# Second phase of a three-stage network in pairs of blocks, with one planned list of operations for both late phases

## The chip, the cores and the metric

The kernel runs on one core of a Trainium2 chip. The metric is the device time of one execution in microseconds (us). Below, PE is TensorE (the matmuls), DVE is VectorE, ACT is ScalarE, POOL is GpSimd, and SP is the engine that issues the transfers.

## The reference

Three stages follow each other. The first is a recurrent attention over 4 batches, 8 heads, 768 positions and 48 channels. Its output, as 3072 tokens of 384 numbers, goes through four experts, each weighted by a probability of the token; the result goes through one more two-layer network with a gate.

```python
p = domain_probs / (domain_probs.sum(-1, keepdims=True) + 1e-09)
for e in range(4):                       # w1: 4 x 384 x 1024, w2: 4 x 1024 x 384
    h = np.maximum(x @ w1[e], 0.0)
    out += p[:, e:e + 1] * (h @ w2[e])
h = out @ w_in                           # 384 x 2048
g = h * np.clip(h + 3.0, 0.0, 6.0) / 6.0
return g @ w_out                         # 2048 x 384
```

w_in and w_out arrive as 64-bit floats.

## The kernel before, in words

**Products.** Every factor is split into a high part and a low part, and a product is three matmuls: high times high, high times low, low times high. A matmul takes 128 rows and 512 tokens.

**Blocks and slices.** The tokens lie in 6 blocks of 512 (NB), the hidden columns in slices of 256 (SL), 16 for the experts and 8 for the last network. The **first phase** does the attention and, in an order written out by hand, the first 7 slices (S0) of the experts for every block, and puts the sums of each expert into DRAM (acc_d). Its last steps, those of block 5, are the tail. The **second phase** does the other 9 slices of the experts (1 of expert 1, 4 each of experts 2 and 3). The **third phase** does the 8 slices of the last network.

**Second phase, block by block.** The loop over steps_ takes one block, one slice and one half of 128 hidden columns at a time, 108 steps. mm1 issues 9 matmuls into ph (line 987), ACT makes the high part of the relu (line 997), DVE the low part (line 1004), and mm2 issues the 9 matmuls of the step before into three sums po (line 1038). After the last step of an expert, finish multiplies each sum by the probability (line 1077) and adds it to the block's accumulator acc (line 1082), both on DVE; add_acc1 (line 1065, DVE) adds what the first phase left. The finished block is stored as x2_d (line 1084).

**The decode.** decode (from line 813) turns w_in and w_out into 32-bit floats in 48 jobs of 256 columns, a job in two steps of the second phase: six DVE instructions (lines 847, 849, 853, 860, 861, 862), and on GpSimd a square (line 848) and an add (line 863).

**Third phase, pairs of blocks.** It takes two blocks at once with a scheme that forms a 2x3 by 3x2 product of tiles with 11 products in place of 12. group is one slice of one pair: 11 products into two PSUM banks, chain_a and chain_b (line 1388), which hold running sums, and 36 second-layer matmuls into six sums pq (line 1432), 69 in all. A chain is copied out on ACT (copied, line 1392) or added to the copy on DVE (summed, line 1396); the gate is four instructions, ACT, DVE, ACT, DVE (lines 1403, 1407, 1416, 1419). The inputs have to be prepared. Sums and differences of the two blocks' tiles (prepare_x, lines 1331 to 1336) and of the weight quarters (prepare_w, lines 1271 to 1274) are made on GpSimd. High parts are made on ACT (lines 1281, 1290, 1350), low parts on DVE (lines 1283, 1292, 1352). Prepared weights are stored in DRAM (ws_d) for the first pair and fetched for the others. The place of each of these in the order is a time written out by hand (at_u), in units of three matmuls, 23 to a group.

**Order.** Each engine works its instructions in the order in which they are issued, and waits in that order. SP issues the loads and stores, GpSimd stands in the same order of issue.

Of the kernel before, what the change touches and what calls it, by code (L numbers as in the profile page):

```python
# [720 lines left out]
def tile_gla__then__moe__then__moe2(  # L721
# [41 lines left out]
    SB = 4  # L763
# [4 lines left out]
    xp = ctx.enter_context(tc.tile_pool(name="xp", bufs=2))  # L768
    rawp = ctx.enter_context(tc.tile_pool(name="rawp", bufs=2))
    wpa = ctx.enter_context(tc.tile_pool(name="wpa", bufs=S0))  # L770
    hp = ctx.enter_context(tc.tile_pool(name="hp", bufs=2))
    gp = ctx.enter_context(tc.tile_pool(name="gp", bufs=2))
    dram = ctx.enter_context(tc.tile_pool(name="dram", bufs=1, space=bass.MemoryType.DRAM))
# [39 lines left out]
    def decode():  # L813

        CW = 256
        big = f32_of((1151 << 20) - 1)
        tiny = f32_of(897 << 20)
        ve = nc.vector  # L820
        jobs = []
        for src, dst in ((w_in, w_in32), (w_out, w_out32)):
            s_ = src.bitcast(I32).rearrange("(p r) c -> p (r c)", p=P)
            d_ = dst.rearrange("(p r) c -> p (r c)", p=P)
            jobs += [(s_, d_, c) for c in range(d_.shape[1] // CW)]
        raws_ = {}

        def load(x):
            if x < len(jobs):
                s_, _, c = jobs[x]  # L830
                raws_[x] = dp.tile([P, CW, 2], I32, tag="raw", bufs=2, name=f"raw_{x}")
                nc.sync.dma_start(raws_[x].rearrange("p n w -> p (n w)"), s_[:, 2 * CW * c : 2 * CW * (c + 1)])

        load(0)
        load(1)
        for _ in range(3):
            yield
        last = None
        for x, (_, d_, c) in enumerate(jobs):
            if x:  # L840
                load(x + 1)
            raw = raws_.pop(x)
            hi, lo = raw.bitcast(F32)[:, :, 1], raw.bitcast(U32)[:, :, 0]
            hc = dp.tile([P, CW], F32, tag="hc", name=f"hc_{x}")
            sq = dp.tile([P, CW], F32, tag="sq", name=f"sq_{x}")
            a = dp.tile([P, CW], F32, tag="a", bufs=2, name=f"a_{x}")
            ve.tensor_scalar(hc, hi, big, -big, op0=ALU.min, op1=ALU.max)  # L847
            nc.gpsimd.tensor_tensor(sq, hc, hc, op=mul)  # L848
            ve.tensor_scalar(
                a.bitcast(I32), hc.bitcast(I32), 3, 0x3FFFFFF8,  # L850
                op0=ALU.logical_shift_left, op1=ALU.bitwise_and,
            )
            ve.scalar_tensor_tensor(
                a.bitcast(I32), hc.bitcast(I32), -0x40000000, a.bitcast(I32),
                op0=ALU.bitwise_and, op1=ALU.bitwise_or,
            )
            if last:
                nc.sync.dma_start(*last)
            yield
            ve.scalar_tensor_tensor(a, sq, tiny * tiny, a, op0=ALU.is_ge, op1=mul)  # L860
            ve.tensor_scalar(hc.bitcast(I32), a.bitcast(I32), -0x800000, None, op0=ALU.bitwise_and)
            ve.scalar_tensor_tensor(hc, lo, 2.0**-52, hc, op0=mul, op1=mul)
            nc.gpsimd.tensor_tensor(a, a, hc, op=add)
            last = (d_[:, CW * c : CW * (c + 1)], a)
            yield
        nc.sync.dma_start(*last)


# [23 lines left out]
    for b in range(NBLK):  # L892
        phase_visits(1, b, S0, S1)
# [8 lines left out]
    def rw(nm):  # L902
        nonlocal nraw
        if early:
            return early.pop(0)
        nraw += 1
        pool = rawq if late and nraw % 3 == 0 else rawp
        return pool.tile([P, 3 * SL], F32, tag="rw", name=nm)
# [21 lines left out]
    def round_w(y, i):  # L930
        raw = raws.pop((y, i))
        pool = wpb if S0 <= i < S0 + SB else wpa
        hi, lo = (pool.tile([P, 3 * SL], F32R, tag=f"w{y}{z}", name=f"w{y}{z}_{i}") for z in "hl")
# [6 lines left out]

    def load_x(phase, n):
        raw = rw(f"rx_{phase}_{n}").rearrange("p (k t) -> p k t", k=KT)
        nc.sync.dma_start(raw, x_d[:, :, n * U : n * U + U])
        raws[(phase, n, "x")] = raw
# [19 lines left out]
    hts, accs, pbs, acc = {}, {}, {}, {}  # L964
    late, rawq = False, None
    halfs, pair, plan = 0, None, {}

    def mm1(vi, f):
# [29 lines left out]
        if plan is not None:  # L998
            plan[(vi, f)] = high
        else:  # L1000
            high()
# [8 lines left out]
    def mm2(vi, f, held=False):  # L1010
# [10 lines left out]
        elif first:  # L1021
            nonlocal ps2
            if ps2 is None:
                ps_ctx.close()
                ps2 = ctx.enter_context(tc.tile_pool(name="ps2", bufs=3, space=PSUM, reuse_waits="tile"))
            second = vv["phase"] == 1 and vi % 2
            pools = [(psa, "psa") if second else (ps2, "ps2") for m in range(KT)]
            accs[vi] = [pool.tile([P, 512], F32, tag=tag, name=f"po_{vi}_{m}") for m, (pool, tag) in enumerate(pools)]
        terms = ((wh, hh), (wl, hh), (wh, hl))
        spans = ((0, 1), (2,)) if half and not last else ((0, 1, 2),)  # L1030
        for m, os in [(m, os) for os in spans for m in range(KT)]:
# [7 lines left out]
            if last and plan is None and not held and (m > 0 or not half):  # L1039
                for x in (0, 1) if half and m == 1 else (m,):  # L1040
                    finish(vi, x)
# [11 lines left out]
    def load_acc(b):  # L1053
        acc[b] = sp.tile([P, KT, NB], F32, tag="acc", name=f"acc_{b}")
        nc.sync.dma_start(acc[b], acc_d[0][:, :, b * NB : (b + 1) * NB])

    def load_acc1(e, n):
        raw = rw(f"ra{e}_{n}").rearrange("p (k t) -> p k t", k=KT)
        nc.sync.dma_start(raw, acc_d[e][:, :, n * U : n * U + U])
        raws[(e, n, "a")] = raw  # L1060

    def add_acc1(e, n):
        b, c = n * U // NB, n * U % NB
        a = acc[b][:, :, c : c + U]
        nc.vector.tensor_tensor(a, a, raws.pop((e, n, "a")), op=add)

    def finish(vi, m):
# [3 lines left out]
        b, t0 = vv["b"], vv["b"] * NB + vv["lo"]  # L1071
        pb = pbs[vi][:, 0:n]
        if vv["phase"] == 0 and m == KT - 1:
            t = pbs[vi]
        else:
            t = gp.tile([P, 512], F32, tag="t", name=f"t_{vi}_{m}")
        nc.vector.tensor_tensor(t[:, 0:n], po[:, 0:n], pb, op=mul)
        if vv["phase"] == 0:
            after(2, lambda: nc.sync.dma_start(acc_d[vv["e"]][:, m, t0 : t0 + n], t[:, 0:n]))
            return  # L1080
        a = acc[b][:, m, :]
        nc.vector.tensor_tensor(a, a, t, op=add)
        if vv["steps"][-1] == (S1 - 1, 1):
            after(1, lambda: nc.sync.dma_start(x2_d[:, m, t0 : t0 + n], a))
# [35 lines left out]

    loads = []
    flying = []
    ended = -1

    def get_w(i):
        for y in range(2):
# [343 lines left out]
    for at_step, (vi, f) in enumerate(steps_):  # L1470
# [13 lines left out]
        if done:  # L1484
            mm2(*done)
# [83 lines left out]
```

## Time and profile before

| | us |
|---|---|
| median of 3 runs (lowest, highest) | 1351.98 (1350.5, 1352.17) |
| profiled execution | 1353.04 |
| span of the profiled execution | 1351.3 |
| PE busy | 1323.3 (98%) |
| DVE busy | 902.2 (67%) |
| ACT busy | 512.2 (38%) |
| GpSimd busy | 144.1 (11%) |
| second phase (518.80 to 959.40 us of the span) | 440.6 |
| third phase (959.40 to 1339.10) | 379.7 |

The span is the part of the execution that the profiler saw, so the two times of that execution differ by 1.7 us. The mean granted clock of TensorE was 0.992 of its full speed, and 1.00 in both late phases. A busy share says how long an engine had an instruction in work; it does not say whether anything waited for it. Which engine was waited for is read from the waits and from the chain that ended last.

### The profile page before, as it was taken

To read this page: it belongs to the slowest core of one execution; us is meant where nothing else is said; L and a number is where in the kernel's file an instruction comes from. 1 tells how busy PE (TensorE), PEld (TensorE's weight loads), DVE (VectorE), ACT (ScalarE), POOL (GpSimd) and SP (SyncE) were. 2 spreads that over 40 slices of the span, in tenths; PEclk is the share of its full clock that TensorE was granted. 3 is DMA by queue.
4 is the path that set the end of the run, shared out by engine and by line. 5 is a ranking of instruction groups with operands and counts; after the bars stand their busy time and mean duration, and the time that the engine had idled before them with its cause. 6 is when DMAs were issued, how large, how long until landed. Compare 5 with 4: busy or idle time off the path is not lost.

```text
span 1351.3 us, 26852 instructions
## 1 busy us (share of the span) xinstructions
PE 1323.3 (98%) x10958; PEld 1103.1 (82%) x10958; DVE 902.2 (67%) x1678; ACT 512.2 (38%) x890; POOL 144.1 (11%) x204
## 2 busy tenths in 40 slices
PE   8899999999999999999999999999999999999996
PEld 7889887888888888888888888888788888888885
DVE  8899977777875377666565756534668655655444
ACT  4654455444444232111121111113456544544442
POOL 4000000000000011111111111112114101100000
PEclk8899999999999999999999999999999999999998
DMA  7765535436252475424251524122565575537313
GB/s 208 199 171 148 159 109 147 139 93 188 78 146 64 138 230 156 131 85 131 65 146 55 156 60 144 47 86 80 196 206 210 216 189 169 168 105 192 125 39 47
DMA packets 177355, 183.13 MB, mean 136 GB/s; under 512 B 74576, under 2 KB 139472, under 8 KB 177232
## 3 DMA queue, kind: packets, MB, share of 16 engines
q1 hardware_dynamic: 173920, 180.83, 44.6%
q8 instruction: 86, 1.41, 0.4%
q10 hardware_dynamic: 3312, 0.59, 0.3%
q14 instruction: 37, 0.30, 0.1%
HBM read 129.94 MB, written 51.43 MB: 134 GB/s over the span
## 4 chain that ended last, share of the span: by engine, by line
PE 91%; DVE 4%; ACT 2%; DMA 1%; issue 1%; SPq 0%; DVEq 0%; ACTq 0%
PE ph L987 29%; PE po L1038 28%; PE pq L1432 14%; PE chain_b L1388 7%; PE chain_a L1388 6%; PE py L628 2%; PE pa L525 2%; PE py L650 1%; PE pu L573 1%; PE py L611 1%; ACT qt L481 1%; DVE kt L513 1%; PE pk L551 0%; DVE hl L1004 0%; PE pkt L468 0%
## 5 line engine op out<-in xcount | busy, mean ns | idle before, releaser
L997 ACT ACTIVATE hh<-ph 128x512 fp32r<-128x512 f32 (+1 forms) x206 | 117.2, 570 | 527.3 <-PE ph L987 518.8
L1004 DVE SCALAR_TENSOR_TENSOR hl<-ph,hh 128x512 fp32r<-128x512 f32 (+1 forms) x206 | 134.0, 651 | 224.3 <-ACT hh L997 221.6
L1038 PE MATMUL po<-hh,w1h 128*128 128x512 f32 (+1 forms) x618 | 233.7, 382 | 0.0
L1038 PE MATMUL po<-hh,w1l 128*128 128x512 f32 (+1 forms) x618 | 229.8, 375 | 0.0
L1038 PE MATMUL po<-hl,w1h 128*128 128x512 f32 (+1 forms) x618 | 224.5, 376 | 3.2 <-DVE hl L1004 3.2
L987 PE MATMUL ph<-xh,w0h 128*128 128x512 f32 (+1 forms) x618 | 168.7, 381 | 2.1 <-DVE hl L1004 1.1
L987 PE MATMUL ph<-xl,w0h 128*128 128x512 f32 (+1 forms) x618 | 165.5, 376 | 0.3 <-issue 0.3
L987 PE MATMUL ph<-xh,w0l 128*128 128x512 f32 (+1 forms) x618 | 165.6, 376 | 0.0
L1038 PEld LDWEIGHTS po<-hh,w1h 128*128 128x128 f32 x618 | 116.2, 188 | 22.7
L1038 PEld LDWEIGHTS po<-hl,w1h 128*128 128x128 f32 x618 | 113.1, 189 | 24.8 <-DVE hl L1004 3.7
L1038 PEld LDWEIGHTS po<-hh,w1l 128*128 128x128 f32 x618 | 116.3, 188 | 20.1
L987 PEld LDWEIGHTS ph<-xh,w0h 128*128 128x128 f32 x618 | 111.3, 189 | 24.9 <-DVE hl L1004 3.1
L987 PEld LDWEIGHTS ph<-xl,w0h 128*128 128x128 f32 x618 | 112.7, 189 | 22.0 <-DVE xl L959 0.6
L987 PEld LDWEIGHTS ph<-xh,w0l 128*128 128x128 f32 x618 | 112.9, 189 | 21.5 <-DVE w0l L936 0.2
L1432 PE MATMUL pq<-hl,pw1h 128*128 128x512 f32 x288 | 112.2, 389 | 0.0
L1432 PE MATMUL pq<-hh,pw1l 128*128 128x512 f32 x288 | 112.0, 389 | 0.0
L1432 PE MATMUL pq<-hh,pw1h 128*128 128x512 f32 x288 | 112.0, 389 | 0.0
L1419 DVE SCALAR_TENSOR_TENSOR hl<-g,hh 128x512 fp32r<-128x512 f32 x96 | 68.9, 717 | 62.7 <-ACT hh L1416 62.6
L848 POOL TENSOR_TENSOR sq<-hc 128x256 f32<-128x256 f32 x48 | 34.5, 718 | 593.4 <-DVE hc L847 591.5
L1396 DVE TENSOR_TENSOR s<-cA,chain_b 128x512 f32<-128x512 f32 x72 | 49.4, 685 | 56.1 <-PE chain_b L1388 40.9
L1416 ACT ACTIVATE hh<-g 128x512 fp32r<-128x512 f32 x96 | 60.8, 633 | 60.4 <-DVE g L1407 60.2
L1403 ACT ACTIVATE g<-s,three 128x512 f32<-128x512 f32 x72 | 52.2, 725 | 81.2 <-DVE s L1396 81.2
(219 smaller groups left out, 2041.3 us busy)
## 6 DMA issues: line engine op xcount, KB each, us to landing
vl<-vd SPq DMA_DIRECT2D x96, 96.0 KB
pb<-p_d SPq DMA_DIRECT2D x28, 256.0 KB
raw<-in_moe_w_in_dram SPq DMA_DIRECT2D x24, 256.0 KB
raw<-in_moe_w_out_dram SPq DMA_DIRECT2D x24, 256.0 KB
pw0h<-ws_d SPq DMA_DIRECT2D x16, 384.0 KB
pw0l<-ws_d SPq DMA_DIRECT2D x16, 384.0 KB
pw1h<-ws_d SPq DMA_DIRECT2D x16, 384.0 KB
pw1l<-ws_d SPq DMA_DIRECT2D x16, 384.0 KB
```

The source lines that it names most:

```text
L525: pe.matmul(pas[h][64 * j : 64 * j + 64, l % 2, r, :], s["kc"][l][64 * h : 64 * h + D, NP * j + r, :], s["qc"][l][64 * h : 64 * h + D, NP ...
L848: nc.gpsimd.tensor_tensor(sq, hc, hc, op=mul)
L987: pe.matmul(ph[:, 0:n], w[:, j, fs], x[:, j, cs], start=(o == 0 and j == 0), stop=(o == 2 and j == KT - 1),)
L997: high = lambda: nc.scalar.activation(hh[:, 0:n], ph[:, 0:n], AF.Relu)
L1004: nc.vector.scalar_tensor_tensor(hl[:, 0:n], ph[:, 0:n], 0.0, hh[:, 0:n].bitcast(F32), op0=ALU.max, op1=sub)
L1038: pe.matmul(accs[vi][m][:, 0:n], w[:, z, ms], h[:, 0:n], **fl)
L1388: pe.matmul(px[bank], a, b, start=first_ and o == 0, stop=o == 2, skip_group_check=True)
L1396: nc.vector.tensor_tensor(cx[(g, o)], cx[(g, nm)], px[bank], op=add)
L1403: nc.scalar.activation(cx[(g, o, "g")], src, AF.Relu, bias=three)
L1416: nc.scalar.activation(hx[(g, o)][0], t, AF.Copy, scale=1.0 / 6.0)
L1419: nc.vector.scalar_tensor_tensor(hl, t, 1.0 / 6.0, hh.bitcast(F32), op0=mul, op1=sub)
L1432: pe.matmul(accs[(pr, y)][m], a, b, start=first_ and x == 0, stop=last_ and x == 2, skip_group_check=True)
```

## The change

The second phase too goes in pairs of blocks with the scheme of 11 products: 3 pairs by 9 slices, 27 groups of 69 matmuls, ahead of the 24 groups of the third phase. Both late phases and the tail of the first phase are written down as one list of operations. Each has an engine, an estimated length, what it depends on, and a time due. PE's order is the written one and sets the due times; schedule goes through the list and gives each engine, whenever it is free, the ready operation that is due first, or lets it wait for one that is due earlier and soon ready. The order of the starts is the order of issue. It stands in for the times written by hand.

The work on the other engines is the third phase's: add_x and add_w prepare inputs and weights, add_copy and add_sum take the chains out. The gate is two instructions in the second phase (relu on ACT, line 1569, low part on DVE, line 1572). At the end of an expert's slices of a pair, add_end multiplies by the probability on DVE; the first expert's products go straight into the accumulator, the others are added to it on GpSimd. add_acc adds what the first phase left, on GpSimd too. The decode's square moves from GpSimd to ACT, and the decode is no longer tied to steps. Pairs 1 and 2 fetch the prepared weights of the second phase from DRAM.

```diff
-    for b in range(NBLK):
-        phase_visits(1, b, S0, S1)
...
-        a = acc[b][:, m, :]
-        nc.vector.tensor_tensor(a, a, t, op=add)
...
-    def add_acc1(e, n):
...
-        nc.vector.tensor_tensor(a, a, raws.pop((e, n, "a")), op=add)
...
+    LAG = dict(PE=260, DVE=120, ACT=120, POOL=150, SP=0, ON=0)
...
+    def dve(n, fn, *deps):
+        return op("DVE", 190 + n * 104 // 100, fn, *deps)
...
+    def pool(n, fn, *deps):
+        return op("POOL", 120 + n * 27 // 10, fn, *deps)
...
+    def schedule():
+        pos = 0
+        for o in ops:
+            if o.eng == "PE":
+                o.due = pos
+                pos += o.dur
+        for o in reversed(ops):
+            d = min(
+                (n_.due - (o.lag if n_.eng != o.eng or o.eng == "SP" else 0) for n_ in o.next), default=pos + 60000
+            ) - o.dur
+            o.due = d if o.due is None else min(o.due, d)
...
+                o = ops[ready[e_][0][1]]
...
+                if hold and e_ != "ON":
+                    free[e_] = min(s_ for _, s_ in hold)
+                    continue
...
+            o3 = act(256, lambda ks=ks, hc=hc: nc.scalar.activation(SQ.place(ks), hc(), AF.Square), o2, ds_)
...
+            o9 = op("POOL", 850, lambda a=a, hc=hc: nc.gpsimd.tensor_tensor(a(), a(), hc(), op=add), o8)
...
+        if pr > 0:
+            sv = saved[(ph, s_)]
+            l0 = dma(500, 1280, lambda: nc.sync.dma_start(rings[0].place(k0).bitcast(F32), wd[s_, :, 0 : 20 * P]), d0, sv[0], later)
+            l1 = dma(500, 768, lambda: nc.sync.dma_start(rings[1].place(k1).bitcast(F32), wd[s_, :, 20 * P :]), d1, sv[1], later)
...
+        if I_[G]["ph"] == 1:
+            a = act(590, lambda: nc.scalar.activation(HR.place(k)[0], get(), AF.Relu), dep, d)
+            b = dve(
+                512,
+                lambda: nc.vector.scalar_tensor_tensor(HR[k][1], get(), 0.0, HR[k][0].bitcast(F32), op0=ALU.max, op1=sub),
+                a,
+            )
...
+                    def f_add(k=k, c=c, ka=ka):
+                        a = AC[k][:, :, c * U : c * U + U]
+                        nc.gpsimd.tensor_tensor(a, a, V(rooms_x[c][ka]), op=add)
...
+            o1 = dve(512, lambda: nc.vector.tensor_tensor(OR.place(k), bank[(y, m)], PR[kp], op=mul), dep, lp, d, opened)
+            o2 = pool(512, lambda: nc.gpsimd.tensor_tensor(AC[ka][:, m], AC[ka][:, m], OR[k], op=add), o1, writes[m])
...
+    for G in range(NG):
+        if G == 0:
+            prev = (final_tail, lambda: None)
+        else:
+            prev = (lambda G=G: add_second(G - 1, 2), lambda G=G: add_second(G - 1, 1))
+        add_group(G, prev)
...
+        if G + 2 < NG:
+            add_w(G + 2)
...
+    for o in schedule():
+        o.fn()
```

PE in the second phase before: one step of block 1. ph is the first layer's sum, po_0 to po_2 the second layer's; xh and xl are the block's input, w0 and w1 the weights (h high, l low).

```order
L987 MATMUL ph_5_8774<-xh_1_8204,w0h_7590 128x512 x3
L987 MATMUL ph_5_8774<-xh_1_8204,w0l_7591 128x512 x3
L987 MATMUL ph_5_8774<-xl_1_8205,w0h_7590 128x512 x3
L1038 MATMUL po_0_8663<-hh_4_8755,w1h_7594 128x512
L1038 MATMUL po_0_8663<-hh_4_8755,w1l_7595 128x512
L1038 MATMUL po_0_8663<-hl_4_8756,w1h_7594 128x512
```

PE in the second phase of the changed kernel: the start of a group of the first pair. X00 to X08 are the pair's prepared inputs, V_0 to V_2 the prepared weights, and sum the six second-layer sums of the pair.

```order
L1534 MATMUL chain_a<-X01h_7444,V_2_8449 128x512 x2
L1534 MATMUL chain_a<-X01l_7449,V_2_8449 128x512
L1534 MATMUL chain_b<-X08h_7458,V_2_8449 128x512 x2
L1534 MATMUL chain_b<-X08l_7467,V_2_8449 128x512
L1534 MATMUL chain_b<-X00h_7439,V_2_8449 128x512 x2
L1534 MATMUL chain_b<-X00l_7446,V_2_8449 128x512
L1619 MATMUL sum_7896<-hh_8559,V_2_8234 128x512 x2
L1619 MATMUL sum_7896<-hl_8560,V_2_8234 128x512
```

The two layers still alternate, but the first layer's sums are now chains that are read out while they are built.

DVE in the second phase before: low parts of h, the two halves of a decode job, a weight slice, an input half and an add of add_acc1.

```order
L1004 SCALAR_TENSOR_TENSOR hl_1_7730<-ph_1_7719,hh_1_7729 128x512
L847 TENSOR_SCALAR hc_7735<-raw_7650 128x256
L849 TENSOR_SCALAR a_7737<-hc_7735 128x256
L853 SCALAR_TENSOR_TENSOR a_7737<-hc_7735,a_7737 128x256
L936 TENSOR_TENSOR w1l_7759<-rw_12_7681,w1h_7758 128x768
L959 TENSOR_TENSOR xl_0_7670<-rx_1_7683,xh_0_7669 128x3x256
L1065 TENSOR_TENSOR acc_7588<-acc_7588,ra_0_7685 128x3x256
L1004 SCALAR_TENSOR_TENSOR hl_2_7783<-ph_2_7772,hh_2_7782 128x512
```

DVE in the changed kernel, in one of the first groups of the second phase: cs is a sum of a chain, X14 to X18 belong to the next pair, da, dhc and dsq to the decode.

```order
L1572 SCALAR_TENSOR_TENSOR hl_8329<-cs_8312,hh_8328 128x512
L1396 TENSOR_TENSOR X14l_8115<-xr_2_8198,X14h_8015 128x256
L1396 TENSOR_TENSOR X18l_8179<-pu_8271,X18h_8021 128x256
L1481 TENSOR_TENSOR V_2_8302<-wr_3_8300,V_2_8302 128x768
L1396 TENSOR_TENSOR X15l_8125<-xr_2_8288,X15h_8051 128x256
L1396 TENSOR_TENSOR X16l_8148<-xr_2_8288,X16h_8066 128x256
L1552 TENSOR_TENSOR cs_8375<-ct_8362,chain_b 128x512
L1396 TENSOR_TENSOR X17l_8173<-pu_8271,X17h_8076 128x256
L1311 TENSOR_SCALAR dhc_8386<-draw_8237 128x256
L1313 TENSOR_SCALAR da_8393<-dhc_8386 128x256
L1488 TENSOR_TENSOR V_2_8380<-wr_4_8254,V_2_8380 128x768
L1572 SCALAR_TENSOR_TENSOR hl_8391<-cs_8375,hh_8390 128x512
```

Between two low parts of h there now stand a sum and the low parts for the next pair and a later slice, and hl reads a sum in SBUF where it read ph.

GpSimd in the second phase before: the decode alone.

```order
L848 TENSOR_TENSOR sq_7491<-hc_7490 128x256
L863 TENSOR_TENSOR a_7492<-a_7492,hc_7490 128x256
L848 TENSOR_TENSOR sq_7572<-hc_7571 128x256
L863 TENSOR_TENSOR a_7573<-a_7573,hc_7571 128x256
L848 TENSOR_TENSOR sq_7653<-hc_7652 128x256
```

GpSimd in the changed kernel, around the end of the second expert's slices of the first pair: da is the decode, wr the weight sums, acc the pair's two accumulators, xr a stored sum of the first phase, o a multiplied sum.

```order
L1643 TENSOR_TENSOR acc_7973<-acc_7973,xr_3_8399 128x3x256
L1326 TENSOR_TENSOR da_8462<-da_8462,dhc_8458 128x256
L1643 TENSOR_TENSOR acc_7973<-acc_7973,xr_4_8506 128x3x256
L1463 TENSOR_TENSOR wr_5_8603<-wr_5_8487 128x256
L1464 TENSOR_TENSOR wr_5_8603<-wr_5_8603,wr_5_8487 128x128
L1466 TENSOR_TENSOR wr_5_8603<-wr_5_8487 128x256
L1465 TENSOR_TENSOR wr_5_8603<-wr_5_8487,wr_5_8603 128x128
L1643 TENSOR_TENSOR acc_7973<-acc_7973,xr_4_8527 128x3x256
L1688 TENSOR_TENSOR acc_7973<-acc_7973,o_8634 128x512
L1688 TENSOR_TENSOR acc_7973<-acc_7973,o_8642 128x512
```

The adds to the accumulators and the weight sums of the second phase are new there, and the squares are gone.

## Rows read from the trace of the kernel before

**Rows 1.** The page, part 1: busy us (share of the span) xinstructions.

```profile
PE 1323.3 (98%) x10958; PEld 1103.1 (82%) x10958; DVE 902.2 (67%) x1678; ACT 512.2 (38%) x890; POOL 144.1 (11%) x204
```

**Rows 2.** Windows: tail, second phase, third phase, end; last three columns clock, DMA share, GB/s.

```profile
461.70:518.80 57.10, 57.10 (x254) 47.28 (x253) 40.55 (x71) 21.74 (x32) 7.52 (x11) 1.00 0.76 224
518.80:959.40 440.60, 440.60 (x1946) 364.83 (x1945) 270.70 (x513) 82.79 (x141) 82.13 (x106) 1.00 0.33 102
959.40:1339.10 379.70, 378.09 (x1666) 312.12 (x1664) 226.13 (x335) 187.42 (x312) 40.89 (x48) 1.00 0.48 155
1339.10:1351.30 12.20, 0.01 (x1) 0.00 (x0) 1.23 (x3) 0.00 (x0) 0.00 (x0) 0.66 0.81 120
```

**Rows 3.** Chain that ended last: start us, us, what; both late phases.

```profile
518.85 2.04 PE ph L987 x9
...
960.17 1.37 PE chain_b L1388 x6
```

**Rows 4.** All waits of PE from 461 to 1340 us: total, times, longest.

```profile
PE chain_a L1388 <- ACT cA L1392: 1.6, 1, 1.6
```

**Rows 5.** Timeline at the border of the late phases: start us, us, [idle before <-releaser].

```profile
964.37 0.74 POOL L1274 TENSOR_TENSOR pc<-pr 128x256 f32<-128x256 f32 x1
...
964.45 1.21 DVE L1082 TENSOR_TENSOR acc<-acc,t 128x512 f32<-128x512 f32 x1
...
967.27 0.59 ACT L1392 COPY cA<-chain_a 128x512 f32<-128x512 f32 x1 [1.21 <-DVE acc L1082]
...
967.90 0.50 PE L1388 MATMUL chain_a<-X,pw0h 128*128 128x512 f32 x1 [1.61 <-ACT cA L1392]
```

**Rows 6.** Groups of DVE from 461 us by form: xcount | busy us, mean ns | idle.

```profile
L1004 DVE SCALAR_TENSOR_TENSOR hl<-ph,hh 128x512 fp32r<-128x512 f32 x123 | 84.8, 689 | 180.2 <-ACT hh L997 180.2
...
L1396 DVE TENSOR_TENSOR s<-cA,chain_b 128x512 f32<-128x512 f32 x72 | 49.4, 685 | 56.1 <-PE chain_b L1388 40.9 <-ACT cA L1392 15.2
L1077 DVE TENSOR_TENSOR t<-po,pb 128x512 f32<-128x512 f32 x60 | 40.7, 682 | 0.1
...
L853 DVE SCALAR_TENSOR_TENSOR a<-hc,a 128x256 int32<-128x256 int32 x48 | 34.5, 719 | 1.6
L862 DVE SCALAR_TENSOR_TENSOR hc<-raw,hc 128x256 f32<-128x256 uint32 x48 | 20.4, 425 | 1.6
...
L861 DVE TENSOR_SCALAR hc<-a 128x256 int32<-128x256 int32 x48 | 14.2, 295 | 1.6
...
L1292 DVE TENSOR_TENSOR pw0l<-pc,pw0h 128x768 fp32r<-128x768 f32 x8 | 7.6, 954 | 0.1
...
L1352 DVE TENSOR_TENSOR X<-pt,X 128x256 fp32r<-128x256 f32 x12 | 4.8, 417 | 0.0
```

**Rows 7.** One line's instructions of the late phases: duration ns min/median/max, first and last start.

```profile
L1407 DVE SCALAR_TENSOR_TENSOR g<-g,s x72: 676/693/1229, 963.1 to 1334.6; 128x512 f32<-128x512 f32 x72
L1407 DVE SCALAR_TENSOR_TENSOR g<-g,chain_a x24: 673/690/690, 973.3 to 1330.4; 128x512 f32<-128x512 f32 x24
...
L1082 DVE TENSOR_TENSOR acc<-acc,t x54: 691/693/1211, 532.2 to 969.8; 128x512 f32<-128x512 f32 x54
```

**Rows 8.** Groups of GpSimd from 461 us by form.

```profile
L863 POOL TENSOR_TENSOR a<-a,hc 128x256 f32<-128x256 f32 x48 | 38.8, 807 | 184.6 <-DVE hc L862 184.6
L848 POOL TENSOR_TENSOR sq<-hc 128x256 f32<-128x256 f32 x48 | 34.5, 718 | 593.4 <-DVE hc L847 591.5 <-DMA raw<-in_moe_w_in_dram 2.0
...
L1334 POOL TENSOR_TENSOR pu<-px,px 128x256 f32<-128x256 f32 x6 | 7.2, 1207 | 4.8 <-DMA px<-x_d 4.8
```

**Rows 9.** Two windows of the third phase.

```profile
1040.00:1055.60 15.60, 15.60 (x70) 12.94 (x69) 12.38 (x16) 8.79 (x15) 9.06 (x10) 1.00 0.64 219
1050.00:1075.00 25.00, 25.00 (x112) 20.72 (x111) 17.04 (x26) 14.95 (x27) 4.54 (x5) 1.00 0.76 284
```

**Rows 10.** Group of ACT's copies of chain_a, from 461 us, by form.

```profile
L1392 ACT COPY cA<-chain_a 128x512 f32<-128x512 f32 x72 | 41.8, 581 | 45.4 <-PE chain_a L1388 44.2 <-DVE acc L1082 1.2
```

**Rows 11.** Table of waits, 518 to 1339 us: waits of ACT for a weight load.

```profile
ACT pw0h L1281 <- DMA pr<-w_in: 4.2, 5, 1.2
```

More of the change, by code (lines that the diff above doesn't have):

```diff
@@ L811, in f32_of @@
         return struct.unpack("<f", struct.pack("<I", bits))[0]
[L813 to L866, printed above, removed]
@@ L997, in mm1 @@
         high = lambda: nc.scalar.activation(hh[:, 0:n], ph[:, 0:n], AF.Relu)
[L998 to L1001, printed above, removed]
+        plan[(vi, f)] = high
         def low():
@@ L1025, in mm2 @@
                 ps2 = ctx.enter_context(tc.tile_pool(name="ps2", bufs=3, space=PSUM, reuse_waits="tile"))
[L1026 to L1028 removed]
+            accs[vi] = [ps2.tile([P, 512], F32, tag="ps2", name=f"po_{vi}_{m}") for m in range(KT)]
         terms = ((wh, hh), (wl, hh), (wh, hl))
@@ new lines, in tile_gla__then__moe__then__moe2, with __init__, new, place @@
+    class Ring:
+        def __init__(self, make, n):
+            self.make, self.n, self.made, self.users = make, n, [], []
+        def new(self):
+            k = len(self.made)
+            self.users.append([])
+            self.made.append(None)
+            before = self.users[k - self.n] if k >= self.n else []
+            order = self.users[k - 1][:1] if k else []
+            return k, list(before) + order
+        def place(self, k):
+            self.made[k] = self.make(k)
+            return self.made[k]
+        def __getitem__(self, k):
+            return self.made[k]
+        def use(self, k, *os):
+            self.users[k].extend(os)
@@ new lines, in tile_gla__then__moe__then__moe2, with room, make @@
+    opened = None
+    NPRE = 2
+    def room(x, tag, shape):
+        later = named(tag, shape)
+        def make(k):
+            return fixed[x] if k < NPRE else later(k)
+        return Ring(make, 1)
+    rooms_x = [room(x, f"xr{x}", [P, 3 * U]) for x in (0, 1, 2)]
+    rooms_w = [room(x, f"wr{x}", [P, 3 * SL]) for x in (3, 4, 5)]
+    room_u = Ring(named("pu", [P, 2 * U], where=late_pool), 1)
+    XT = [
+        [[Ring(named(f"X{par}{x}{z}", [P, NB], F32R, where=None if par else late_pool), 1) for z in "hl"] for x in range(9)]
+        for par in range(2)
+    ]
@@ new lines, in tile_gla__then__moe__then__moe2, with open_more @@
+    for s_, fn in todo:
+        dma(400, 256, fn)
+    add_x(0)
+    pend_, hl_ops, gone = list(pend), [], []
+    for x, (vi, f) in enumerate(tail):
+        hl_ops.append(tail_first(vi, f, *(hl_ops[x - 2] if x >= 2 else [])))
+        done = tail_second(*pend_.pop(0))
+        if done and x == 0:
+            dma(500, 256, lambda: load_p(len(visits) - 1), done)
+        pend_.append((vi, f))
+    add_w(0)
+    add_w(1)
+    def open_more():
+        nonlocal more
+        old.close()
+        more = ctx.enter_context(tc.tile_pool(name="more", bufs=1, reuse_waits="tile"))
```

912 lines of the change are left out of this document (576 added, 336 removed).

## The prediction

> **What bounds the kernel now.** I read the page's busy table first. TensorE (PE) works 1323.3 of 1351.3 us, VectorE (DVE) two thirds of it, GpSimd (POOL) a tenth [rows 1]. A busy share is a mean over stages, so I cut the span at the stage borders: the second phase takes 440.6 us and PE is busy in all 440.60 of them, the third 379.7 with 378.09 busy, and the last 12.2 us have no matmul that counts [rows 2]. In the table of waits PE stands still once in the two late phases, for 1.6 us [rows 4]. So here PE's stream of matmuls is the time, and only two things can change it: how many matmuls there are, and whether PE begins to wait.
>
> The chain of waits gives the price of a matmul. A first layer of 9 takes 2.04 us, and a piece of six of the pair scheme, which the third phase already uses, 1.37 [rows 3]: 0.227 us each, in either phase. The second phase checks it: 108 steps of 18 at 0.227 make 440.6.
>
> **What it removes.** A step of the second phase serves one block and half a slice (128 hidden columns) with 18 matmuls, so one slice for a pair of blocks took four steps, 72. As a group it takes 33 + 36 = 69. There are 3 pairs and 9 slices, 27 groups, so 81 matmuls go: 81 x 0.227 = **-18.4 us**. The second phase becomes 422.3 us and a group 15.64 us. Nothing covers this work, so it counts in full.
>
> **The one wait that goes.** The timeline around 967 us shows what PE waited for. DVE's add to the sums took 1.21 us there, where the shortest takes 0.69, while GpSimd ran beside it; ScalarE's (ACT) copy of chain_a came 1.21 us late and PE stood 1.61 us [rows 5, 7]. In the changed order this add is on GpSimd and is not in front of the sums of a new phase: **-1.6 us**. If it stays, the sum is 1.6 higher.
>
> **What it adds.** The pair scheme wants prepared inputs: sums of input blocks and of weight quarters on GpSimd, high parts on ACT, low parts on DVE, a copy of chain_a on ACT and a sum on DVE. In PE's rows these are now inside every group of the second phase. I count what the new order gives each engine and price it by rows of before.
>
> DVE, all of the second phase: 108 low parts of h at 0.69, 81 sums at 0.69, 48 multiplications at 0.68, 63 low parts of X at 0.417, 48 decode jobs at 2.14 (two with two inputs at 0.425, three with one input at 0.295, and the one of 0.719 at 0.425 too, because GpSimd's square no longer runs beside it) and the low parts of ten slices at some 2.7 (256 columns cost 0.417 and 768 cost 0.954, so 384 about 0.55 and 128 about 0.28) [rows 6]. That makes 321 us of 422, 76%, against 270.7 of 440.6 before [rows 2]. ACT, by the same count, has some 170 us of 422 and does not bind.
>
> It is not even. In the second to fourth group (46.9 us) DVE gets 9 sums, 12 low parts of h, 6 multiplications, 18 low parts of X, 15 low parts of weights and three to four decode jobs: 43 us, 92%. From the fifth group on it is 10 to 14 of 15.64. Windows of one group's length with 12.38 us of DVE and 9.06 of GpSimd left PE 15.60 of 15.60 busy [rows 9]. So up to about 13 us of DVE per group I cost at nothing, hidden beside PE. Above that lie groups 2 to 4, a few later ones where the next pair's inputs are made, and the first group of the third phase.
>
> **GpSimd beside DVE** is the term that before shows only in part. The same DVE instruction over the same columns takes 690 ns at most when one input is chain_a in PSUM, and up to 1229 when both are in SBUF; the add, also with both in SBUF, has 691 at the least and 1211 at the most [rows 7]. On the other side GpSimd's sum of 256 columns takes 807 ns in the decode and 1207 in the sums of inputs [rows 8]. So two instructions that both read SBUF take turns, and one with a PSUM input does not care. The change gives GpSimd in the second phase 48 decode adds, 30 adds of 512 columns, 24 of 768, and the sums for ten slices and seven half-pairs of inputs. In units of 256 columns that is some 254, and at 0.72, the length of the decode's square [rows 8], about 183 us, where the second phase showed 82.13 [rows 2].
>
> Of DVE's 321 us about 115 are instructions with two SBUF inputs besides hl, and 75 are hl, three quarters of which now read an SBUF sum instead of PSUM. In the dense groups some 20 us of GpSimd fall on 29.6 us of such DVE work in 46.9. Lower bound: they find the gaps, 0 us, as in the windows of [rows 9]. Upper bound: each GpSimd instruction there puts its whole length, times the share of DVE time that can be hit, on DVE, and what exceeds 15.64 per group goes to PE: summed over the groups 27 us (3 to 4 in each of groups 2 to 4, 6, 10 and 19, the rest in small amounts). Half of the overlaps gives 6; since a group can work ahead for the next I take **+5 us**, nearer the lower end, because the nearest rows, the windows, lie there.
>
> Here the Trainium skill bears on the change ("SBUF — State Buffer", section "Who interferes with whom"): a VectorE instruction with two SBUF inputs shares a port with GpSimd's reads, and whoever issues first keeps it for the whole instruction. The rows on chain_a and s agree in kind. By that rule alone, every overlap in full, the sum would be the upper bound, 1360, not 1338.
>
> **Moving the adds.** 54 adds of 512 columns cost DVE at least 0.69 each before [rows 7]; 30 of them and 24 of 768 columns are now GpSimd's, at about 1.44 and 2.15 us by the 0.72 of [rows 8]. GpSimd's sums are due a group or more ahead, and its adds are waited for only at a segment's end and at the handover to the third phase, so I cost them at nothing beyond the term above. Its cover is the four output buffers of the multiplications; if it fails, DVE's next multiplication waits and with it PE's banks.
>
> The Trainium skill's "GPSIMD Engine Reference", section "4.1 Engine selection", puts a two-input add on VectorE, about twice as fast. The rows agree. It would make the sum worse only where GpSimd is waited for, and I have found no such place.
>
> **Inputs.** The bytes of the second phase, counted from the code (prepared weights of 2 MB stored nine times and fetched 18 times, decode, raw weights, partial sums), come to 108 MB, 255 GB/s over 422 us, against 102 before [rows 2]. A window of 25 us at 284 GB/s left PE 25.00 of 25.00 busy [rows 9]; the longest wait of ACT for a weight load was 1.2 us [rows 11]. Lower bound 0, upper bound a wait of that size in each of the 27 groups, 32. I take 0: fetches are two groups ahead.
>
> **The sum.** The profiled execution took 1353.04, 1.06 above the median of the runs: 1353.04 - 18.4 - 1.6 + 5 = 1338.0, and 1337 against the median. 0.2% (2.7 us) is about what a measurement of this kernel tells from no change.
>
> **Rivals.**
> - **Copies late (1344).** In a group the second product of chain_a waits for ACT's copy of the first, 0.58 us [rows 10], and in DVE's new rows a decode instruction of up to 0.72 [rows 6] can stand ahead of a sum. One late copy of 0.45 per group, 27 times, gives 12 us less saved instead of 5. For it: the wait of [rows 4] is of this kind. Against: the same order ran 24 groups in the third phase with that one wait. It decides from 0.2 us per group.
> - **DVE and GpSimd take turns throughout (1359): the slower case.** The upper bound above, 27 us, with no room to work ahead: 1353.0 - 20 + 27 = 1360, 1359 to the median. For it: DVE at 92% in the dense groups and rows that show 1.2 for 0.69. It turns slower when the added delay on PE's path passes 20 us. Against: the windows with 9 us of GpSimd.
> - **No gain (1352).** The 20 us go at the border of the first and second phase and in the first groups, where the inputs for a pair are made out of block 5's outputs, or in late fetches at 255 GB/s. For it: both were idle work hidden before. Against: 57.10 us of old steps of PE lie there to hide them [rows 2].
> That the change does less than it says is excluded: the new order has exactly 69 matmuls per group.
>
> **How the numbers follow.** Forecast 1337 with 0.70 (its own range 1332 to 1343), copies late 0.14, no gain 0.07, taking turns 0.09. The first two lie faster by over 0.2%: 0.84. The low end is the sum without any added wait, 1331.9 against the median, so 1331; up to 1349 the range takes in the second case and part of what lies between it and no gain, and leaves out about 0.16.
>
> **What would show it.** Right: the second phase near 423 to 430 us, PE busy in nearly all, 69 matmuls per 15.64 us, the wait at the phases' border gone, DVE near 76% there, GpSimd twice its time. PE's waits, if any, stand in groups 2 to 4 with DVE's sums or ACT's copies as releasers. Wrong: PE waiting on a DMA of V tiles (inputs), on hl or sums in most groups at some 0.45 us (copies), or GpSimd's adds of 512 columns at over 2 us with DVE near 100% (turns).

## The result and the profile after

The changed kernel took 1367.45 us in the median of four runs (1365.37 to 1369.2), the kernel before 1352.08: a ratio of 1.0116, 95% interval 1.0097 to 1.0134. It is slower by 1.2%, where 1337 was forecast. The profiled execution took 1369.2.

The page's busy line of the changed kernel, to be held against [rows 1], and its windows for the second phase and for the third phase with the end of PE's work, against [rows 2]:

```profile
PE 1327.5 (97%) x10877; PEld 1089.2 (80%) x10877; DVE 982.0 (72%) x1771; ACT 594.7 (43%) x1097; POOL 264.6 (19%) x288
```

```profile
522.16:970.00 447.84, 440.43 (x1882) 352.83 (x1882) 365.80 (x636) 172.77 (x343) 196.24 (x186) 1.00 0.73 244
970.00:1356.00 386.00, 382.58 (x1648) 309.97 (x1646) 222.24 (x331) 183.26 (x308) 38.38 (x43) 1.00 0.46 144
```

The second phase was to shrink from 440.6 to 422.3 us and grew to 447.8. By the page PE is busy in all but some 7 us of it, so most of the 25.5 us that are missing against the forecast are not idle time. The chain that ended last shows a part of them:

```profile
527.66 1.39 PE chain_b L1534 x6
...
530.41 2.10 PE sum L1619 x9
```

Nine matmuls now take 2.10 us and six 1.39, against 2.04 and 1.37 in [rows 3]. The third phase is slower too, though the change takes no matmul from it and adds none: its groups have a mean spacing of 229 to 232 ns. (The spacing is the time from the start of one matmul to the start of the next; it is shorter than a matmul's own duration, since they overlap.) A second measure needs two rows of the instructions by line (duration in ns min/median/max, first and last start): the first product of the late phases and their last matmul.

```profile
L1534 PE MATMUL chain_a<-X01h,V x52: 388/391/506, 522.0 to 1207.4; 128*128 128x512 f32 x52
L1619 PE MATMUL sum<-hl,V x612: 388/394/629, 530.7 to 1354.7; 128*128 128x512 f32 x153
```

From 522.0 to 1354.7 are 832.7 us. Between these two starts lie 51 groups of 69 matmuls and nine of the tail, 3527 steps, which at 0.2267 us, the mean spacing of the kernel before, would take 799.6. So 33.1 us are lost. Summed over all pairs of neighbouring matmuls less than 0.26 us apart, the slower spacing makes 14.9 of them, with a mean of 231 ns; the other 18.2 are stops and what follows them. PE's table of waits over the late phases names 9.8 of these (ct is ACT's copy of chain_a, cs DVE's sum of ct and chain_b):

```profile
PE chain_b L1534 <- DVE cs L1552: 5.1, 6, 2.5
PE chain_a L1534 <- ACT ct L1544: 4.7, 5, 2.5
```

Of the rest, 6.0 are steps of over 0.26 us with no gap between the matmuls, most of them right behind a stop, and 2.3 are the parts of stops that lie under the end of the matmul before. Behind each of the two largest stops, at 630 and 984 us, the granted clock is at the lower of its two levels, 1.2 GHz, for some 3 us (the column before the last two in this window):

```profile
633.90:636.90 3.00, 3.00 (x9) 2.32 (x8) 2.30 (x3) 1.85 (x3) 2.71 (x3) 0.50 0.56 155
```

Some 11 of the 18 us lie in groups 3 to 7, 4 in the second group of the third phase. The profiled execution also came 3 us later into the second phase (522.0 against 518.85). In the eight profiles of experiments on the changed kernel the second phase began between 516.7 and 519.3, so these 3 us are not the change's; this execution was the slowest of the four.

One stop, in the timeline of 630 us:

```profile
630.05 1.81 POOL L1643 TENSOR_TENSOR acc<-acc,xr 128x768 f32<-128x768 f32 x1
630.13 1.88 DVE L1311 TENSOR_SCALAR dhc<-draw 128x256 f32<-128x256 f32 x1 [0.63 <-POOL da L1326]
...
632.04 0.42 ACT L1312 ACTIVATE dsq<-dhc 128x256 f32<-128x256 f32 x1 [5.02 <-DVE dhc L1311]
632.37 0.57 ACT L1544 COPY ct<-chain_a 128x512 f32<-128x512 f32 x1
...
632.99 0.73 PE L1534 MATMUL chain_a<-X06h,V 128*128 128x512 f32 x2 [2.48 <-ACT ct L1544]
```

GpSimd begins its add of 768 columns 0.08 us before DVE begins an instruction of the decode that usually takes 0.29, and DVE ends 0.15 us after GpSimd. The decode's square waits for it on ACT; the copy of chain_a stands behind the square in ACT's order, and PE waits 2.48 us for the copy. The other large stop, at 984 us, is of the same kind, with one of GpSimd's adds of 512 columns and one of DVE's weight parts, which usually takes 0.96:

```profile
983.99 1.72 POOL L1688 TENSOR_TENSOR acc<-acc,o 128x512 f32<-128x512 f32 x1
...
984.50 2.02 DVE L1481 TENSOR_TENSOR V<-wr,V 128x768 fp32r<-128x768 f32 x1
```

How far DVE's instructions are stretched in the second phase (min/median/max):

```profile
L1572 DVE SCALAR_TENSOR_TENSOR hl<-cs,hh x80: 672/692/2333, 527.6 to 956.9; 128x512 fp32r<-128x512 f32 x80
L1572 DVE SCALAR_TENSOR_TENSOR hl<-chain_a,hh x27: 674/683/692, 534.5 to 959.0; 128x512 fp32r<-128x512 f32 x27
...
L1311 DVE TENSOR_SCALAR dhc<-draw x48: 278/292/1941, 559.8 to 937.2; 128x256 f32<-128x256 f32 x48
```

### The profile page after: what moved, and what is told of

The parts are those of the page before. It is cut to its first block, busy times and chain, and to the rows that moved or that the text cites. A ratio compares the mean times of both kernels' runs of the same rounds, so it can differ in the third digit from the quotient of the medians.

```text
span 1367.5 us, 27179 instructions
## 1 busy us (share of the span) xinstructions
PE 1327.5 (97%) x10877; PEld 1089.2 (80%) x10877; DVE 982.0 (72%) x1771; ACT 594.7 (43%) x1097; POOL 264.6 (19%) x288
## 3 DMA queue, kind: packets, MB, share of 16 engines
q8 instruction: 85, 1.39, 0.4%
## 4 chain that ended last, share of the span: by engine, by line
PE 77%; DVE 11%; DMA 3%; POOL 2%; ACT 2%; issue 2%; SPq 1%; DVEq 0%; ACTq 0%; POOLq 0%
PE sum L1619 25%; PE chain_b L1534 13%; PE ph L923 11%; PE chain_a L1534 11%; PE po L969 9%; PE po L1797 2%; PE py L628 2%; DMA wr<-in_moe_w_dram 1%; PE pa L525 1%; PE py L650 1%; DMA w_out<-da 1%; POOL acc L1688 1%; DVE cs L1552 1%; PE pu L573 1%; POOL acc L1643 1%
## 5 line engine op out<-in xcount | busy, mean ns | idle before, releaser
L1619 PE MATMUL sum<-hh,V 128*128 128x512 f32 x1224 | 383.7, 395 | 0.0
L1619 PEld LDWEIGHTS sum<-hh,V 128*128 128x128 f32 x1224 | 231.0, 189 | 53.2
L1619 PE MATMUL sum<-hl,V 128*128 128x512 f32 x612 | 241.0, 394 | 0.0
L1552 DVE TENSOR_TENSOR cs<-ct,chain_b 128x512 f32<-128x512 f32 x153 | 104.7, 684 | 100.4 <-PE chain_b L1534 75.3
L1619 PEld LDWEIGHTS sum<-hl,V 128*128 128x128 f32 x612 | 115.4, 189 | 27.3 <-DVE hl L1572 0.4
L969 PE MATMUL po<-hh,w1h 128*128 128x512 f32 (+1 forms) x249 | 90.7, 372 | 0.0
L969 PE MATMUL po<-hh,w1l 128*128 128x512 f32 (+1 forms) x249 | 86.6, 356 | 0.0
L969 PE MATMUL po<-hl,w1h 128*128 128x512 f32 (+1 forms) x249 | 80.6, 355 | 3.3 <-DVE hl L937 3.3
L923 PE MATMUL ph<-xh,w0h 128*128 128x512 f32 (+1 forms) x294 | 77.8, 374 | 3.5 <-ACT xh L893 2.1
L923 PE MATMUL ph<-xh,w0l 128*128 128x512 f32 (+1 forms) x294 | 74.7, 363 | 0.0
```

The costliest lines, as they stand in the source:

```text
L923: pe.matmul(ph[:, 0:n], w[:, j, fs], x[:, j, cs], start=(o == 0 and j == 0), stop=(o == 2 and j == KT - 1),)
L969: pe.matmul(accs[vi][m][:, 0:n], w[:, z, ms], h[:, 0:n], **fl)
L1552: o = dve(512, lambda: nc.vector.tensor_tensor(SR.place(k), CR[kc], chain[1], op=add), dep, oc, d)
L1619: pe.matmul(bank[(y, m)], a, b, start=first_ and x == 0, stop=last_ and x == 2, skip_group_check=True)
```

## The experiments

Two theories came out of this. For the spacing: it depends on where a matmul's two operands lie, the moving one (the tokens) and the stationary one (the weights). In the built program of the kernel before, every moving and every stationary tile of the last 3600 matmuls starts at 160 modulo 256 bytes of its partition. The changed kernel has a pool (late) that is filled from the other end of SBUF, whose tiles start at 224. Its spacing repeats with the address, not with the load of the other engines: in the third phase, groups of the same pair and the same place of three for their weights agree within a few tenths of a ns. For the stops: GpSimd's long adds hold DVE. The rivals are late loads, and work that comes late because it is queued on GpSimd.

The runs were made in several sets, each with the kernel before beside it, whose median went from 1352.08 to 1354.85. So kernels of different sets are compared by the ratio.

| kernel | median us | ratio to before (95%) | first product to last matmul, us |
|---|---|---|---|
| changed | 1367.45 | 1.0116 (1.0097 to 1.0134) | 832.7 |
| e1 aligned | 1355.1 | 1.0007 (0.9996 to 1.0018) | 821.3 |
| e3 aligned, adds on DVE | 1340.28 | 0.9904 (0.9885 to 0.9923) | 806.4 |
| e4 aligned, later loads | 1352.98 | 0.9998 (0.9987 to 1.0009) | 819.9 |
| e5 as e3, idle adds on GpSimd | 1353.67 | 0.9997 (0.9983 to 1.0011) | 818.8 |
| e5 as e3, idle memsets on GpSimd | 1339.94 | 0.9899 (0.9876 to 0.9922) | 805.4 |
| e7 as e3, weights in one piece, later decode | 1334.63 | 0.9855 (0.9835 to 0.9874) | 801.0 |
| e8 as e3, weights in one piece | 1334.17 | 0.9853 (0.9835 to 0.9871) | 800.4 |
| e9 as e7, five rounds | 1334.17 | 0.9854 (0.9838 to 0.9869) | 800.4 |

**Alignment.** e1 puts one unused tile of 64 bytes under the late pool.

```diff
+    ctx.enter_context(tc.tile_pool(name="shift", bufs=1, side="right")).tile([P, 16], F32, tag="shift", name="shift")
     late_pool = ctx.enter_context(tc.tile_pool(name="late", bufs=1, side="right", reuse_waits="tile"))
```

> The changed kernel with one unused tile of 64 bytes a partition below the right-hand pools, so that every moving and stationary tile of the late phases starts at 160 modulo 256 bytes of its partition (in the changed kernel 59% of the moving and 35% of the stationary addresses of the last 3600 matmuls do, the others start at 224). The order of the instructions is the same. Theory of addresses: a matmul whose moving and stationary addresses differ modulo 256 costs 233 ns in place of 226.7, so spacing returns to 226.7 everywhere and the 15 us of slow spacing go: about 1352. Rival, that transfers or the other engines slow the matmuls: spacing stays at 231 on the mean and the time at 1367.

The chain and the table of waits of e1:

```profile
655.49 1.36 PE chain_b L1534 x6
656.85 2.04 PE sum L1619 x9
```

```profile
PE chain_b L1534 <- DVE cs L1552: 7.3, 7, 2.9
PE chain_a L1534 <- ACT ct L1544: 5.6, 6, 2.8
```

Nine matmuls are back at 2.04 us; the mean spacing over both phases is 226.9 ns. The ratio falls by 1.1%, 15 us. The stretch from the first product to the last matmul falls by 11.4 only: PE arrives earlier in this profile, and the stops grow from 18 to 21 us. Every engine has the same instructions in the same order as in the changed kernel, and no transfer was relieved, so the slow spacing was the addresses.

**How far may the operands lie apart?** In the kernel before, the weights of four slices are shifted by some bytes; their order stays. The list gives a shift in elements of 4 bytes. The tiles also become 128 bytes wider, which moves those of slices 8 and 10 by 128 bytes more; the shifts below are taken from the built program.

```diff
-        hi, lo = (pool.tile([P, 3 * SL], F32R, tag=f"w{y}{z}", name=f"w{y}{z}_{i}") for z in "hl")
+        x_, o_ = (32, (4, 8, 16, 0)[i - S0]) if pool is wpb else (0, 0)
+        hi, lo = (pool.tile([P, 3 * SL + x_], F32R, tag=f"w{y}{z}", name=f"w{y}{z}_{i}")[:, o_ : o_ + 3 * SL] for z in "hl")
```

> The kernel before with the weight tiles of four of the nine slices of the second phase shifted against their moving tiles: slice 7 by 16 bytes, slice 8 by 160, slice 9 by 64, slice 10 by 128; slices 11 to 15 stay. Theory of addresses: the 864 matmuls of the shifted slices, or those of some of the shifts, take up to 233 ns in place of 226.7 and the others none, at most 5.7 us, about 1358; which shifts cost tells how wide the line is. Rival: spacing stays 226.7 in every slice, 1352.

The second kernel has (8, 16, 12, 28) in place of (4, 8, 16, 0).

> The kernel before with other shifts of the same four slices' weights: slice 7 by 32 bytes, slice 8 by 192, slice 9 by 48, slice 10 by 240. In the first set 16 bytes cost nothing and 64, 128 and 160 gave 233 ns. Theory of lines of 64 bytes from 160 less 32: 32 and 48 cost (the start leaves the line at 192), 192 costs, 240 costs. Theory of lines of 32 bytes: the same for 32 and 48; 240 lies one line before and costs. Theory of a distance that matters only from 64 bytes on: 32, 48 and 240 (16 bytes below) cost nothing, only 192 does. Time by spacing: 216 matmuls of 6.6 ns a slice, 1.4 us for each slice that costs, 1353 to 1358.

The chain in block 1 of the first of the two, each row the first layer of a slice's first step: slice 7 (shift 16), 8 (160), 9 (64), 10 (128).

```profile
595.85 2.04 PE ph L988 x9
...
604.02 2.10 PE ph L988 x9
...
612.42 2.10 PE ph L988 x9
...
620.80 2.08 PE ph L988 x9
```

The same of the second: slice 7 (32), 8 (192), 9 (48), 10 (240).

```profile
594.67 2.10 PE ph L988 x9
...
603.03 2.07 PE ph L988 x9
...
611.33 2.10 PE ph L988 x9
...
619.69 2.06 PE ph L988 x9
```

A shift by 16 bytes costs nothing: in the first kernel every spacing in slice 7 is 226 or 227 ns, up to where matmuls of slice 8 stand among its own; from there on those of slice 7 take 230 to 237. Shifts of 32, 48, 64, 128 and 160 cost about 6 ns a matmul, 192 (64 bytes below) about 3, and 240 (16 bytes below) under 2. Unshifted slices stay at 226.7, but for the first ones behind a shifted slice. The changed kernel agrees: where the weights lie 64 bytes above the moving tile (modulo 256) the mean is 233.4 ns, where they lie 64 below 230, and where both lie alike 229, with the first ones behind others among them. It also answers a rival that the shifts leave open, that the address of one operand alone matters: behind nine matmuls with both operands at 224 the mean is 227.4 ns, and with both at 160 it is 227.1. The times are single executions, 1360.53 and 1358.83, against 1353 for the kernel before; they lie 2.5 and 0.8 us over what was expected at most, so the verdict here rests on the spacing. The theory of a distance that matters only from 64 bytes on is out. Both others had 240 cost like 32, and that is not borne out: 16 bytes below cost 1.2 ns, 32 above 6.4.

**GpSimd's adds.** e3 moves the adds to the accumulators to DVE, in add_acc and add_end.

```diff
-                        nc.gpsimd.tensor_tensor(a, a, V(rooms_x[c][ka]), op=add)
+                        nc.vector.tensor_tensor(a, a, V(rooms_x[c][ka]), op=add)
-                    o = pool(3 * U, f_add, writes[:KT], l2)
+                    o = dve(3 * U, f_add, writes[:KT], l2)
-            o2 = pool(512, lambda: nc.gpsimd.tensor_tensor(AC[ka][:, m], AC[ka][:, m], OR[k], op=add), o1, writes[m])
+            o2 = dve(512, lambda: nc.vector.tensor_tensor(AC[ka][:, m], AC[ka][:, m], OR[k], op=add), o1, writes[m])
```

> The aligned kernel with the 24 adds of 768 columns and the 30 (36 with the pairs' ends) adds of 512 columns on VectorE in place of GpSimd, the list put in order again. Theory that GpSimd's long adds hold VectorE: VectorE instructions of 1.8 to 2.3 us vanish, PE's waits in the second phase fall from some 14 us to under 6, 8 to 10 us less than the aligned kernel, though VectorE works some 43 us more. Rival, that late weight loads and the issue queue make the waits: the waits stay, and with VectorE at some 86% of the phase they grow; the aligned kernel's time or up to 10 us more.

PE's waits in the late phases, and the decode's instruction again:

```profile
PE chain_a L1534 <- ACT ct L1544: 2.2, 4, 1.6
PE sum L1619 <- DVE hl L1583: 0.6, 1, 0.6
PE chain_b L1534 <- DVE cs L1552: 0.2, 1, 0.2
```

```profile
L1311 DVE TENSOR_SCALAR dhc<-draw x48: 279/289/820, 555.1 to 945.7; 128x256 f32<-128x256 f32 x48
```

15 us less than e1, although DVE does 60 adds more (24 of 768 columns and 36 of 512). The longest of L1311 fell from 1929 ns in e1 to 820. To see whether it is the adds' reads that hold DVE, or work that is queued behind them on GpSimd, two kernels give GpSimd idle work behind each of DVE's adds: an add as wide as before, or memsets that take as long and read nothing.

```diff
+                    o3 = pool(3 * U, lambda c=c, ka=ka: nc.gpsimd.tensor_tensor(V(rooms_x[c][ka]), V(rooms_x[c][ka]), V(rooms_x[c][ka]), op=add), o)
...
+            o3 = pool(512, lambda: nc.gpsimd.tensor_tensor(OR[k], OR[k], OR[k], op=add), o2)
```

> The aligned kernel with the adds on VectorE (1340.3), and on GpSimd, behind each of them, an add of the same width on the buffer that has just been used up: its result is read by nobody. Theory that GpSimd's reads hold VectorE: VectorE instructions of 1.8 to 2.3 us come back and with them 10 us or more: 1350 to 1362 (VectorE keeps the 43 us of adds too). Second theory, that work queued behind GpSimd's long instructions comes late (the decode's adds, the weight sums): also 1350 or more. Rival, that only the place of the true adds mattered: 1340.

```diff
+                    o3 = pool(3 * U, lambda c=c, ka=ka: [nc.gpsimd.memset(rooms_x[c][ka][:, 0:n_], 0.0) for n_ in (768, 768, 256)], o)
...
+            o3 = pool(512, lambda: [nc.gpsimd.memset(OR[k][:, 0:n_], 0.0) for n_ in (512, 512, 256)], o2)
```

> The same, but the work added on GpSimd only writes: three memsets of 768, 768 and 256 columns (some 1.8 us by the rows of 0.53 us for 512 columns) in place of an add of 768, and of 512, 512 and 256 (1.4 us) in place of an add of 512. GpSimd is busy as long. Theory that GpSimd's reads hold VectorE: no VectorE instruction is held, about 1340, within 3 us of the kernel with the adds on VectorE. Second theory, that what is queued on GpSimd comes late: as with the adds, 1350 or more.

With idle adds, waits of PE and the decode's instruction:

```profile
PE chain_b L1534 <- DVE cs L1552: 6.0, 10, 1.2
PE chain_a L1534 <- ACT ct L1544: 3.9, 7, 1.6
```

```profile
L1311 DVE TENSOR_SCALAR dhc<-draw x47: 279/289/1553, 556.5 to 953.3; 128x256 f32<-128x256 f32 x47
```

With idle memsets:

```profile
PE chain_a L1534 <- ACT ct L1544: 2.8, 3, 1.7
PE chain_b L1534 <- DVE cs L1552: 0.7, 1, 0.7
```

```profile
L1311 DVE TENSOR_SCALAR dhc<-draw x48: 277/289/830, 555.4 to 947.3; 128x256 f32<-128x256 f32 x48
```

Adds that nobody reads cost some 13 us (0.9904 to 0.9997); memsets of the same length cost nothing (0.9899). GpSimd was busy about as long in both, 192 and 197 us from 523 to 960 us, and DVE, ACT, PE and SP have the same instructions in the same order. So the queue on GpSimd is out, and what holds DVE is that the adds read. The Trainium skill ("SBUF — State Buffer", section "Who interferes with whom") says that a VectorE instruction with two SBUF inputs shares a port with GpSimd's reads and not with its mere writes, and it lists tensor_scalar, with one input, among those that can take both ports. The runs agree on each: hl with cs, in SBUF, as its second input took up to 2333 ns in the changed kernel and from chain_a, in PSUM, never over 692; L1311 took up to 1941; and the memsets cost PE nothing.

**Late loads.** e4 gives transfers more time in the plan.

```diff
-        o.lag = 2600 + 12 * kb
+        o.lag = 4200 + 12 * kb
```

> The aligned kernel with the planner's time for a transfer at 4.2 us plus 12 ns a KB in place of 2.6 plus 12 (a 256 KB load is then planned at 7.3 us; in the changed kernel such loads landed 3 to 8 us after their issue). Theory of late loads: ScalarE no longer stands before a weight cast (18.3 us in five waits, the longest 5.3), and PE's waits in the second phase fall from some 14 us to under 6: 8 to 10 us less than the aligned kernel. Rival, GpSimd holding VectorE: the waits stay and so does the aligned kernel's time, within 3 us.

ACT's wait for these weights in the second phase, 18.3 us in five waits in the changed kernel and 18.5 in e1, is nearly gone, but PE's waits are not:

```profile
PE chain_b L1534 <- DVE cs L1552: 6.5, 5, 1.6
PE chain_a L1534 <- DVE V L1481: 5.0, 4, 2.8
```

The time is e1's, within some 2 us. While GpSimd holds DVE, loads are not what comes last. Once it doesn't, they are: in e3 the third to fifth group still lose 6 us, with ACT standing up to 3.7 us before a first weight. That weight comes in two pieces, and the second is issued only after the first has landed. e7 and e8 issue them one behind the other; e7 also starts the decode after the sixth group.

```diff
-        l0 = [dma(900, 256, lambda: f_r0(0), da, dec0, later)]
-        if ph == 1:
-            l0.append(dma(500, 128, lambda: f_r0(1), da, l0[0], later))
+        l0 = [dma(1400, 384, lambda: (f_r0(0), ph == 1 and f_r0(1)), da, dec0, later)]
```

> The aligned kernel with the adds on VectorE, and two edits of the list: the two pieces of a slice's first weights are issued one behind the other in place of the second after the first has landed (ScalarE stood 3.7 us before such a weight in the third and fourth group), and the decode begins after the sixth group, not after the first. Theory that the 6 us left in groups 3 to 5 come of late loads on top of a full VectorE: they go, 1334 to 1336. Rival, that they come from elsewhere (the inputs of the next pair): 1340.

> The aligned kernel with the adds on VectorE and the two pieces of a slice's first weights issued one behind the other, the decode as in the changed kernel. Theory that the late second piece alone held the third to fifth group: as with both edits, 1334 to 1336. Theory that VectorE is too full there with decode work: the waits of groups 3 to 5 stay in large part, 1338 to 1340.

> The kernel with all four edits (aligned tiles, adds on VectorE, weights in one piece, decode after the sixth group) once more, in five rounds: 1334 to 1336, 18 to 19 us under the kernel before on the same chip. Its floor by the rows is the kernel before less 18.4 for 81 matmuls and less 1.6 for one wait.

All of PE's waits in the late phases of e9, its second phase, and its first product and last matmul:

```profile
PE chain_a L1532 <- ACT ct L1542: 0.4, 1, 0.4
```

```profile
523.20:947.00 423.80, 423.39 (x1867) 350.21 (x1867) 346.35 (x655) 170.71 (x336) 104.26 (x129) 1.00 0.76 254
```

```profile
L1532 PE MATMUL chain_a<-X01h,V x52: 389/389/389, 518.3 to 1174.3; 128*128 128x512 f32 x52
L1617 PE MATMUL sum<-hl,V x612: 388/389/500, 526.9 to 1318.7; 128*128 128x512 f32 x153
```

800.4 us, 0.8 over the 799.6 of a stream without stops. The loads issued one behind the other do it alone (e8): ACT's wait for these weights, 12.5 us in e3, is gone there. The later decode adds nothing, so a VectorE too full in these groups, the rival, is out: in e8 it is as busy as in e3 (355.6 and 354.2 us from 523 to 947 us). e7, e8 and e9 beat the changed kernel and the one before: 0.9854 is 20 us.

## Why the prediction was wrong

**81 matmuls, -18.4, and one wait, -1.6: right as a floor.** e8 and e9 take 20 us off, and these two terms are 20.0. In the changed kernel itself the wait came back: the stop of 2.5 us at 984 us stands near the same border and has the same cause, a DVE instruction stretched beside GpSimd.

**The step that failed first is the price of a matmul**, "0.227 us each, in either phase". It was read from a kernel whose tiles all lie at one address modulo 256 and carried to tiles that lie elsewhere. It was 231 ns on the mean in both late phases: some 15 us that have no term in the sum and no rival. The new pool stands in the change's code; the rows of before could not show what it does, since they hold no operand at another distance.

**The term of GpSimd beside DVE was mis-sized**: +5, with 27 as its upper bound, where 13.9 go with the adds alone (1.0007 in e1, 0.9904 in e3). It was put near the lower end because windows of the third phase with 9 us of GpSimd showed no wait. Those windows had short sums, ten in 9.06 us; an add of 768 columns holds DVE for 1.8 us at a time, and in the stop shown above PE stood 2.48 us for it. And the account left out the decode's one-input instructions, "two instructions that both read SBUF take turns" read as two inputs only: L1311 was held up to 1941 ns. GpSimd's work itself came much as counted, 196 us against 183, adds of 1.41 and 1.85 us against 1.44 and 2.15. DVE's did not: 365.8 us in the second phase against 321.

**Moving the adds "at nothing beyond the term above"** was the costly edit. It was right that PE waits for none of the adds' results; what was held was DVE, beside them.

**Inputs at nothing: wrong by some 7 us**, once the adds are off GpSimd (0.9904 in e3, 0.9853 in e8), and not by bandwidth: 254 GB/s in e9 leave PE without a wait of over 0.4 us. It was one load issued after another had landed.

**The sum with these sizes.** The addresses took 14.7 us (1.0116 to 1.0007), the adds 13.9 and the loads 6.9, each measured with those before it mended. With them in place of the 5, the forecast of 1337 becomes 1367.5; 1367.45 was measured.

**The rivals.** Of the rivals, the mechanism of "taking turns" (1359, 0.09) came, at half its size: 13.9 us with the adds, not 27, and its own signs did not show, since the adds of 512 columns took 1.41 us in the median, not over 2, and DVE was busy 82% of the second phase. That the time lay nearest to this rival's is in part chance, as the slow spacing and the loads made more than half of the loss. "Copies late" named one of the two last links of the stops, not their cause: PE waits 4.7 us for ACT's copies and 5.1 for DVE's sums, and in the stop shown the copy is held by a square that waits for DVE.

**What stays open:** why the spacing follows the distance of the operands in this way, why a slow matmul slows those beside it, and whether the period is 256 bytes. Shifts beyond 240 weren't tried. The 60 adds were moved together, so what those of 768 and of 512 columns cost each is not known.

## What to carry to other kernels

When a change moves tiles to another pool or another end of SBUF, compare the start addresses of the moving and the stationary operands before trusting the old price of a matmul; one pad tile of 64 bytes was worth 15 us here. Before giving adds to GpSimd because it is idle, look at what DVE does beside them: here one long GpSimd add stretched DVE instructions with two operands in SBUF, and some with a single one, to about its own length, and with orders fixed ahead that stretch travelled over ACT to PE. A load that waits for another to land, without needing it, should be issued with it.

## What the runs showed of the hardware that had not been expected

- The spacing of 512-column matmuls with a new stationary operand each is 226.7 ns when both start at the same place modulo 256 bytes or the stationary one 16 bytes above, 232 to 233.4 ns for distances of 32, 48, 64, 128 and 160 bytes, about 230 for 192 and about 228 for 240. The Trainium skill ("TensorE: Matmul & The Clock Gate", section "Step-by-step: what each phase is for") says that the two operands have independent read ports, so that loading the next weights takes nothing from a running matmul. The measurement does not fit that as it stands: the distance of the two operands' addresses costs up to 3%. By what way, the runs do not show.
- A one-input DVE instruction of 256 columns that takes 0.29 us took up to 1.94 beside GpSimd's adds of 768 columns, and no longer beside memsets (0.83) than without them (0.82).
- Behind a stop of PE of 2.5 us the granted clock fell to 0.50 of full speed, 1.2 of 2.4 GHz, though PE was at work again: for some 3 us the matmuls started 0.43 us apart.
